# A spread of gating jobs over TensorE's order, switched off in a list schedule

## The chip, the cores and the metric

The kernel runs on one core of a Trainium2 chip. The metric is the time of one execution in microseconds; several executions are made and their median is taken. A hardware profile of one execution shows what each engine did: TensorE (PE, with its weight loads as PEld), VectorE (DVE), ScalarE (ACT), GpSimd (POOL), SyncE (SP, which here only issues transfers) and the 16 DMA engines.

## The reference

A gated linear recurrence over 4 sequences of 5,824 tokens with 256 channels, and behind it a multiplicative feed-forward network (FFN) of width 1,024 on all 23,296 tokens.

```python
log_a = c * sig_r * np.log(np.clip(a_base, 1e-06, 1.0 - 1e-06))[None, None, :]
a_t = np.exp(log_a)
norm = np.sqrt(np.maximum(1.0 - a_t * a_t, 1e-06))
x_gated = norm * sig_i * x
for t in range(S):
    h = a_t[:, t] * h + x_gated[:, t]
    y[:, t] = h
...
a = x @ w1
b = x @ w2
h = a * b @ w3
return (h @ w_out).astype(np.float32)
```

Here `sig_r` and `sig_i` are sigmoids of the two gates, and the `x` of the network is the recurrence's `y`.

## The kernel before

**Chunks.** The tokens are cut into 46 chunks: one of 256 tokens and 45 of 512 (L48). Each chunk goes through two halves.

**The gating half.** Three loads on SP's queue bring r, i and x (`load`, L106). ScalarE takes the tanh of both gates (`tanh_r`, `tanh_i`). GpSimd adds 1 and multiplies by x (`plus`, `times`). Two transposes bring channels onto partitions (`turn_r`, `turn_u`; for chunks from 7 on they are DMA transposes issued by SP, L162). ScalarE makes the decay with two exponentials (`decay`, L170), GpSimd squares it (`square`, L177), ScalarE takes the root (`root`, L182), VectorE multiplies (`gated`, L187) and runs the recurrence in two scans, one for each half of the channels (`scan`, L202). GpSimd casts the result to bf16 as `y_t` (`cast`, L210).

**The FFN half.** For each of four column blocks `mp`, TensorE makes `pa` and `pb` in PSUM (`up`, L218), ScalarE copies `pa` to `sa` (`copy`, L225), VectorE multiplies `sa` by `pb` into `g_t` (`product`, L232). Then TensorE multiplies by the folded product of w3 and w_out (`down`, L239), ScalarE copies the result out of PSUM (`evac`, L245) and SP stores it (`store`). `pa` and `pb` share three PSUM buffers (tag `pab`, L67), so TensorE can be no more than three blocks ahead of `copy` and `product`. The text calls the FFN half of chunk c "row c"; its four products are p0 to p3.

**Groups.** tanh and exponential use one ScalarE table and the root another. So the roots of a group of chunks (`group_sizes`, L53: groups of four from chunk 10 on) stand together, and each group costs two table loads. The groups from chunk 10 on begin at chunks 10, 14, 18, 22, 26, 30, 34, 38 and 42.

**The order.** A list schedule in Python (L293 to L500) decides the program order on every engine before the program is built. Each step is a job with an engine, an assumed duration and a due time; at each moment an engine takes the first job, in order of due time, that is startable: inputs done, buffer free. Engines then execute their queues strictly in this order. `EVEN = 10` (L85) adds one more condition for groups whose first chunk is at least 10: the dictionary `hold` (L326 to L348) names, for each gating job, a matmul job that must have begun first (L436). For ScalarE's gating jobs these are spread, in proportion to their durations, over the sixteen `pa` jobs of four rows; for `gated`, the two `scan`s and `cast` of chunk c they are the `pb` jobs 0 to 3 of row c − 2 (`AHEAD = 2`).

```python
        total = sum(d for d, _ in ops)
        acc = 0.0
        for d, key in ops:
            pos = first + min(npos - 1, int(npos * (acc + d / 2) / total))
            hold[key] = ("pa", pos // 4, pos % 4)
            acc += d
        for c in g:
            for mp, key in enumerate((("gated", c), ("scan", c, 0), ("scan", c, 1), ("cast", c))):
                hold[key] = ("pb", c - AHEAD, mp)
```

Of the kernel before, what the change touches and what calls it, by code (L numbers as in the profile page):

```python
# [20 lines left out]
def kernel(  # L21
# [60 lines left out]

    T = {}

    EVEN = 10  # L85
    AHEAD = 2
    NPE = 7
    NDV = 3
# [238 lines left out]
    for k, g in enumerate(groups):  # L327
        if g[0] < EVEN:
            continue
# [205 lines left out]
```

## Time and profile before

| what | us |
|---|---|
| median of 7 executions (572.45 to 574.19) | 573.51 |
| the profiled execution, whole | 573.51 |
| its span, first to last instruction | 571.7 |
| TensorE busy | 502.7 |
| ScalarE busy | 463.1 |
| VectorE busy | 456.4 |
| GpSimd busy | 322.3 |
| first `sa` copy of row 9 | 145.7 |
| first `sa` copy of row 41 | 511.8 |

The span is what the profile shows; 1.8 us of the execution's time lie around it. The last two lines mark the stretch in which the gating of the groups that begin at chunks 10 to 38 meets the FFN: the gated steps and scans of the group that begins at chunk g stand in rows g − 1 to g + 2. Row starts are found by counting `sa` copies, four to a row.

### The profile page before, as it was taken

The numbers are of one execution on the slowest core, as the hardware profiler recorded it, in microseconds if no ns is written. First come the engines' busy times: TensorE is split into PE (matmuls) and PEld (weight loads), VectorE is DVE, ScalarE is ACT, GpSimd is POOL, SyncE is SP. The second block draws the span as 40 slices with busy tenths as digits, with TensorE's granted clock in tenths as the row PEclk, the third lists the DMA queues.
The fourth block names the chain that finished last, engine by engine and source line by source line (L and its number), as shares of the span: only waits on it lengthen the run. The fifth ranks groups of instructions, "written<-read, shape, count | busy, mean of one in ns | idle before, by whom it ended". The sixth has DMA issues, their size and how long they took to land.

```text
span 571.7 us, 8497 instructions
## 1 busy us (share of the span) xinstructions
PE 502.7 (88%) x3104; PEld 304.2 (53%) x3160; DVE 456.4 (80%) x355; ACT 463.1 (81%) x539; POOL 322.3 (56%) x196
## 2 busy tenths in 40 slices
PE   1479898978987999998997997898999899789997
PEld 1346665644654655655554554564565565455565
DVE  1877468497899799799699699789879879978852
ACT  6696899997986988988987897798889799666543
POOL 6124975769197268449558649707926937821000
PEclk9989999989999999999999999999999999999999
DMA  9996799999988859949979989797995993321112
GB/s 219 253 308 179 198 332 253 289 258 246 282 234 229 231 162 277 285 135 272 238 222 250 221 250 205 224 249 184 278 275 148 239 284 106 91 56 56 37 56 92
DMA packets 183897, 120.10 MB, mean 210 GB/s; under 512 B 86576, under 2 KB 182832, under 8 KB 183856
## 3 DMA queue, kind: packets, MB, share of 16 engines
q1 hardware_dynamic: 179216, 115.89, 75.8%
q0 software_dynamic: 4368, 3.67, 3.9%
q8 instruction: 24, 0.39, 0.3%
q14 instruction: 17, 0.14, 0.1%
q10 hardware_dynamic: 272, 0.00, 0.0%
HBM read 78.91 MB, written 23.86 MB: 180 GB/s over the span
## 4 chain that ended last, share of the span: by engine, by line
PE 41%; DVE 20%; issue 14%; ACT 4%; POOL 1%; DVEq 0%; POOLq 0%; ACTq 0%
PE pa L218 15%; PE pb L218 13%; PE po L239 13%; DVE h_t L202 9%; DVE g_t L232 9%; DVE nrm L187 2%; ACT L170 1%; ACT sa L225 1%; ACT ot L245 1%; ACT a_t L170 1%; POOL y_t L210 1%; ACT nrm L182 0%; ACT L182 0%; DVEq L232 0%; POOLq L210 0%
## 5 line engine op out<-in xcount | busy, mean ns | idle before, releaser
L232 DVE TENSOR_TENSOR g_t<-sa,pb 128x1024 bf16<-128x1024 bf16 (+1 forms) x184 | 218.0, 1197 | 70.5 <-ACT sa L225 49.9
L225 ACT CAST sa<-pa 128x1024 bf16<-128x1024 f32 (+1 forms) x184 | 183.8, 1002 | 79.5 <-PE pa L218 73.0
L218 PEld LDWEIGHTS <-w_sb 128*128 128x128 bf16 x1472 | 143.7, 98 | 187.1 <-issue 33.8
L218 PE MATMUL pa<-y_t,w_sb 128*128 128x512 bf16 (+1 forms) x706 | 186.0, 379 | 37.8 <-DVE g_t L232 26.5
L218 PE MATMUL pb<-y_t,w_sb 128*128 128x512 bf16 (+1 forms) x710 | 185.3, 379 | 2.1 <-ACT sa L225 0.6
L239 PE MATMUL po<-wp_sb,g_t 128*128 128x256 bf16 x1456 | 182.8, 274 | 4.4 <-ACT ot L245 3.8
L239 PEld LDWEIGHTS <-g_t 128*128 128x128 bf16 x1456 | 143.2, 98 | 50.5 <-issue 4.9
L202 DVE TENSOR_TENSOR_SCAN h_t<-a_t,h_t,nrm 128x512 f32<-128x512 f32 (+3 forms) x90 | 156.8, 1751 | 0.7
L210 POOL CAST y_t<-h_t 128x1024 bf16<-128x1024 f32 x44 | 55.0, 1250 | 132.5 <-DVE h_t L202 132.5
L177 POOL TENSOR_TENSOR nrm<-a_t 128x1024 f32<-128x1024 f32 x43 | 90.4, 2105 | 31.7 <-ACT a_t L170 31.7
L144 POOL TENSOR_TENSOR u_t<-th_i,x_t 128x1024 bf16<-128x1024 f32 x39 | 97.5, 2500 | 2.8
L132 POOL TENSOR_SCALAR th_i<-th_i 128x1024 f32<-128x1024 f32 x43 | 61.2, 1422 | 46.6 <-ACT th_i L127 45.6
L187 DVE SCALAR_TENSOR_TENSOR nrm<-nrm,ut 128x1024 f32<-128x1024 f32 x39 | 67.7, 1737 | 12.7 <-ACT nrm L182 12.7
L245 ACT COPY ot<-po 128x512 f32<-128x512 f32 x91 | 53.0, 585 | 12.6 <-PE po L239 12.5
L170 ACT ACTIVATE a_t<-rt,la 128x512 f32<-128x512 bf16 x78 | 62.1, 816 | 0.1
L127 ACT ACTIVATE th_i<-i_t 128x1024 f32<-128x1024 f32 (+1 forms) x46 | 48.2, 1047 | 1.3 <-DMA i_t<-in_i_gate_dram 1.3
L182 ACT ACTIVATE nrm<-nrm 128x1024 f32<-128x1024 f32 (+1 forms) x46 | 47.2, 1053 | 2.4 <-DVE nrm L177 1.2
L120 ACT ACTIVATE th_r<-r_t 128x1024 bf16<-128x1024 f32 x39 | 41.4, 1064 | 0.0
L182 ACT ACT_TABLE_LOAD x15 | 19.2, 1283 | 0.3
L152 PE MATMUL ptr<-ident,th_r 128*128 128x128 bf16 x52 | 4.8, 245 | 12.8 <-DVE ident L73 8.7
L170 ACT ACT_TABLE_LOAD x12 | 15.4, 1283 | 0.8 <-DVE la L285 0.6
L187 DVE SCALAR_TENSOR_TENSOR nrm<-nrm,ptr 128x1024 f32<-128x1024 f32 (+1 forms) x7 | 8.0, 1137 | 5.9 <-ACT nrm L182 5.9
(33 smaller groups left out, 103.7 us busy)
## 6 DMA issues: line engine op xcount, KB each, us to landing
out_dram<-ot SPq DMA_DIRECT2D x91, 256.0 KB, 3.2
r_t<-in_r_gate_dram SPq DMA_DIRECT2D x45, 512.0 KB, 5.3
i_t<-in_i_gate_dram SPq DMA_DIRECT2D x45, 512.0 KB, 5.3
x_t<-in_x_dram SPq DMA_DIRECT2D x45, 512.0 KB, 5.2
w_t<-in_moe_w_dram POOLq DMA_DIRECT2D x8, 256.0 KB, 17.0
w_sb<-in_moe_w_dram POOLq DMA_DIRECT2D x8, 128.0 KB, 9.9
rt<-th_r SPq DMA_TRANSPOSE x39, 4.3
ut<-u_t SPq DMA_TRANSPOSE x39, 4.6
```

What stands on the lines that cost most here:

```text
L132: nc.gpsimd.tensor_scalar(t, t, 1.0, 1.0, op0=ALU.add, op1=ALU.mult)
L144: nc.gpsimd.tensor_mul(out=u.rearrange("p cb j q -> p j cb q"), in0=cut(t), in1=cut(T["x", c]))
L170: nc.scalar.activation(out=T["a", c][:, cb, :w], in_=T["pr", c][:, cb, :w], func=AF.Exp, scale=la4[:, cb:cb + 1], bias=la4[:, cb:cb + 1])
L177: eng.tensor_mul(out=t[:, :, :w], in0=T["a", c][:, :, :w], in1=T["a", c][:, :, :w])
L182: nc.scalar.activation(out=T["n", c][:, :, :w], in_=T["n", c][:, :, :w], func=AF.Sqrt, scale=-1.0, bias=1.0)
L187: nc.vector.scalar_tensor_tensor(out=T["n", c][:, :, :w], in0=T["n", c][:, :, :w], scalar=1e-3, in1=T["pu", c][:, :, :w], op0=ALU.max, op1 ...
L202: nc.vector.tensor_tensor_scan(T["h", c][:, cb, lo:hi], T["a", c][:, cb, lo:hi], T["n", c][:, cb, lo:hi], init, ALU.mult, ALU.add)
L210: eng.tensor_copy(out=T["y", c][:, :, :w], in_=T["h", c][:, :, :w])
L218: nc.tensor.matmul(out=pp[:, q, :w], lhsT=w_sb[:, cb, m * P:(m + 1) * P], rhs=T["y", c][:, cb, :w], start=(cb == 0), stop=(cb == NCB - 1))
L225: nc.scalar.copy(out=sa[:, :, :w], in_=T["pa", c, mp][:, :, :w])
L232: nc.vector.tensor_mul(out=T["g", c][:, 2 * mp:2 * mp + 2, :w], in0=T["sa", c, mp][:, :, :w], in1=T["pb", c, mp][:, :, :w])
L239: nc.tensor.matmul(out=T["po", c, j // 2][:, j % 2, :], lhsT=T["g", c][:, k, j * P:(j + 1) * P], rhs=wp_sb[:, k, :], start=(k == 0), stop= ...
```

## The change

The constant goes from 10 to 100. There are 46 chunks, so no group qualifies any more, `hold` stays empty, and the condition at L436 never applies. Nothing else differs: the same jobs with the same durations and due times are scheduled.

```diff
-    EVEN = 10
+    EVEN = 100
```

The same instructions come out on every engine; up to row 8 their order is the same too. Behind it, VectorE's order per group is this, from the group's first gated step to its last scan (g a gated step, s a scan, p an FFN product; the spaces are only for reading):

```
before, groups at 10, 26:  g p p g s p s p s p g p s p s p s p g p s p s
before, groups at 14, 30:  g p s p g p s p s p g p s p p s s p p g s p p s
before, groups at 18, 34:  g s p p g s p p s g p p s p s p g s p p s s
before, groups at 22, 38:  g p g p s s p p s g p p s s p p s g p s p s
after, group at 10:        g p p g s p s p g p s p s p g p s p s p s p s
after, groups at 14, 18:   g p s p g p s p g p s p s p g p s p s p s p s
after, groups at 22 to 38: g s p p g s p g p s p s p g p s p s p s p s
```

The order before repeats every 16 chunks, the order after (from chunk 22) every four. On ScalarE the changed order from chunk 22 on has, in the row of the roots, the first exponential of the next group ahead of that row's last `sa` copy; and `tanh_r` and `tanh_i` of the group's second chunk stand one row later than before in most groups. GpSimd's order changes little: in some groups `times` and `square` of neighbouring chunks swap. SP's loads, transposes and stores keep their number and move by a few places among each other.

## The prediction

> **What bounds the kernel now.** I read the page's busy shares first, then its chain of waits.
>
> ```profile
> PE 502.7 (88%) x3104; PEld 304.2 (53%) x3160; DVE 456.4 (80%) x355; ACT 463.1 (81%) x539; POOL 322.3 (56%) x196
> PE 41%; DVE 20%; issue 14%; ACT 4%; POOL 1%; DVEq 0%; POOLq 0%; ACTq 0%
> PE pa L218 15%; PE pb L218 13%; PE po L239 13%; DVE h_t L202 9%; DVE g_t L232 9%; DVE nrm L187 2%; ACT L170 1%; ACT sa L225 1%; ACT ot L245 1%; ACT a_t L170 1%; POOL y_t L210 1%; ACT nrm L182 0%; ACT L182 0%; DVEq L232 0%; POOLq L210 0%
> ```
>
> The chain runs through TensorE, and where it leaves TensorE it goes mostly to VectorE's scans and products. ScalarE is as busy as VectorE but hardly on the chain. So I cut the stretch from row 9 to row 41 into its eight groups and asked for the busy time of each engine in each; columns are window, length, then PE, PEld, DVE, ACT, POOL.
>
> ```profile
> 145.70:192.20 46.50, 41.34 (x245) 24.13 (x248) 42.42 (x32) 39.32 (x48) 29.80 (x16) 1.00 0.83 228
> 192.20:237.30 45.10, 42.82 (x257) 25.38 (x260) 39.09 (x29) 39.58 (x48) 28.41 (x16) 1.00 0.94 247
> 237.30:282.00 44.70, 42.18 (x255) 25.05 (x258) 38.24 (x28) 39.41 (x48) 29.62 (x16) 1.00 0.84 222
> 282.00:328.10 46.10, 42.27 (x257) 25.21 (x260) 39.70 (x30) 39.19 (x48) 29.45 (x16) 1.00 0.90 236
> 328.10:374.50 46.40, 41.38 (x245) 24.08 (x248) 42.32 (x30) 39.27 (x47) 29.80 (x16) 1.00 0.85 221
> 374.50:419.60 45.10, 42.82 (x257) 25.37 (x261) 39.08 (x29) 39.58 (x48) 28.41 (x16) 1.00 0.95 239
> 419.60:464.30 44.70, 42.17 (x255) 25.05 (x258) 38.27 (x30) 39.41 (x47) 29.62 (x16) 1.00 0.87 228
> 464.30:511.80 47.50, 41.41 (x249) 24.43 (x253) 42.33 (x29) 36.57 (x45) 25.96 (x14) 1.00 0.44 121
> ```
>
> These are the groups at 10, 14, ... 38; together 366.1 us. The same order takes the same time twice (46.5 and 46.4, 45.1 and 45.1, 44.7 and 44.7), so an order has a price. The length follows DVE's busy time: 42.4 goes with 46.5, 38.2 with 44.7. ScalarE's is alike in the first seven, whatever the length.
>
> Why does DVE's busy time differ, with equal work? The timeline inside the group at 26 (start, duration, engine) shows it:
>
> ```profile
> 350.66 1.19 DVE L232 TENSOR_TENSOR g_t<-sa,pb 128x1024 bf16<-128x1024 bf16 x1
> 351.67 2.35 POOL L144 TENSOR_TENSOR u_t<-th_i,x_t 128x1024 bf16<-128x1024 f32 x1
> 351.77 3.33 DVE L187 SCALAR_TENSOR_TENSOR nrm<-nrm,ut 128x1024 f32<-128x1024 f32 x1
> 355.02 1.21 DVE L232 TENSOR_TENSOR g_t<-sa,pb 128x1024 bf16<-128x1024 bf16 x1
> 355.96 1.89 POOL L177 TENSOR_TENSOR nrm<-a_t 128x1024 f32<-128x1024 f32 x1
> 356.16 2.77 DVE L202 TENSOR_TENSOR_SCAN h_t<-a_t,h_t,nrm 128x512 f32<-128x512 f32 x1
> 358.85 1.19 DVE L232 TENSOR_TENSOR g_t<-sa,pb 128x1024 bf16<-128x1024 bf16 x1
> 359.86 2.35 POOL L144 TENSOR_TENSOR u_t<-th_i,x_t 128x1024 bf16<-128x1024 f32 x1
> 359.97 3.32 DVE L202 TENSOR_TENSOR_SCAN h_t<-a_t,h_t,nrm 128x512 f32<-128x512 f32 x1
> ```
>
> A gated step takes 1.22 us and a scan 1.28 alone (their medians), a product 1.2 always. Here POOL starts a step of 1.9 to 2.35 us during each product, just before DVE starts its gated step or scan, and that one lasts until POOL's step is over and its own time has passed on top: 3.33 = 2.25 + 1.1. Undisturbed, a group's DVE work is 16 × 1.21 + 4 × 1.22 + 8 × 1.28 = 34.5 us; the table's mean is 40.2. So 5.7 us of each group are such waits, and where they are many, products and the PSUM buffers behind them come late and TensorE waits.
>
> **The change part by part.** *Instructions.* None is added or removed: the kernels hold the same jobs. All cost lies in the order, from row 9 on; what comes ahead (145.7 us) costs 0.
>
> *VectorE.* What differs among the orders listed with the change is how often a gated step or scan stands right behind a single product, the place where the timeline shows the long waits. Counted per group of 12 such steps, single-product places are 9 in the orders of 46.5 and 46.4 us, 6 at 45.1, 2 at 44.7, but 4 at 46.1 and 47.5. The changed order has 9 in the group at 10, 11 in those at 14 and 18, and 8 in those at 22 to 38, whose last eight steps alternate strictly with products, as in the group at 26. The nearest row is therefore the order with 9: (46.5 + 46.4) / 2 = 46.45 a group, and eight make 371.6. Against 366.1 that is **+5.5 us**. The bounds are the cheaper rows: 45.1 × 8 = 360.8, or −5.3; and the dearest, 47.5 × 8 = 380.0, or +13.9. I take 46.4, rounded down since 8 is a little under 9: 371.2, **+5.1**.
>
> *ScalarE.* A group's work is 8 tanh at 1.06, 8 exponentials at 0.816, 4 roots at 1.05, 16 copies at 1.0, 8 evacuations at 0.585 and 2 table loads at 1.283: 8.5 + 6.5 + 4.2 + 16.0 + 4.7 + 2.6 = 42.5, in either kernel. Moved ahead of the last `sa` copy in the roots' row are a table load and an exponential, 1.28 + 0.82 = 2.1 us. The product behind that copy comes 2.1 us later, but in VectorE's changed order a gated step (1.22) stands ahead of it, and by the next row's first copy both orders have done the same set. So I take 0; uncovered, it is 2.1 − 1.22 = 0.9 a group, +7 over eight. One new wait: `tanh_r` of the group's second chunk now stands a copy (1.0), a tanh (1.07), an evacuation (0.6) and a copy (1.0) ahead of its exponential, 3.7 us, and the DMA transpose between them lands 4.3 us after its issue. The exponential can wait 0.6 us, and behind it in ScalarE's queue the other exponential and the row's last copy. VectorE, late by its waits there, covers it; I take 0, at most 0.6 × 6 = +3.6.
>
> *SP, DMA, POOL.* Loads land in a median of 5.3 us, and ScalarE waited 1.3 us in all for loads of i; with the same buffers and moves of a few places I take 0, up to 5.3 once if a load becomes late. POOL's swaps of a 2.35 and a 1.89 us step are in the group's price. *The last group.* From row 41 to the end takes 571.7 − 511.8 = 59.9 us, TensorE busy nearly throughout. The group at 42 alternates once in the changed order, and POOL's products and squares are over by then, so its scans run at 1.28 us: 0, within 1.5 either way.
>
> *Sum.* 573.5 + 5.1 = **578.6 us** for an execution of which the profiled one, 573.51, is the median of the seven.
>
> **The rivals.** *The alternation does no harm (faster).* At the start of each row the changed order has finished the same VectorE steps as the orders at 18 and 34, the cheapest; only the places inside a row differ, and a product after each step frees PSUM buffers sooner. Then groups cost 45.1 (the order with 6 single places) or less: 360.8 in all, 573.5 − 5.3 = 568.2 us; at 44.7 it is 565.0. For it: single places alone don't order the rows (6 is cheaper than 4). Against: both orders that alternate over long runs are among the dear ones. It decides if POOL has no step ready when the lone product ends.
>
> The Trainium skill bears on this rival: its page "SBUF — State Buffer", section "Who interferes with whom", has VectorE steps with two SBUF inputs and GpSimd steps exclude each other, whichever began first for the whole instruction. With POOL's phase taken as even, a wait behind a product is half a POOL step (an estimate: 0.8 us, from 1.04, 2.35, 1.89 and 1.04) and behind another such VectorE step a whole one, 1.6. Counting places, the changed order from 22 on would then wait 2 × 1.6 + 10 × 0.8 = 11.2 us a group and the old ones on average 3 × 1.6 + 9 × 0.8 = 12.0; by 1.75 us of length for 4.1 of DVE time (first and third row above) that is −0.3 a group, 571 us. The trace agrees with the exclusion (3.33 us) but not with the even phase: POOL began 0.10 to 0.20 us ahead of the waiting step three times in a row. I go by the row.
>
> *Nothing measurable.* A reshuffle without a better or worse order on average: eight groups at the mean of 45.8, 573.5 us. For it: the four old orders are themselves a mixture, and the work is the same. Against: the new order is one order repeated, and single orders differ by 2.8 us.
>
> *ScalarE too.* The 2.1 us ahead of the last copy and the late exponential are not covered, and come on top of VectorE's waits: 47.5 a group, 587.4 us. Against: the old profile shows VectorE waiting for `sa` 49.9 us in all, mostly in rows without gating.
>
> **How the numbers follow.** Within 0.2%, 1.1 us either way, I call it the same, about what measurements of this kernel can tell. The forecast with its neighbours above 574.7 has 0.52, ScalarE too 0.10, nothing measurable 0.13, the faster rival (with the even phase) 0.25. So slower 0.62, same 0.13, faster 0.25. Since cases of both signs hold most of the chance: the forecast's own range is 575 to 583 (46.0 to 46.9 a group). For 8 in 10 the range reaches down to 569.0, which cuts off the cheaper half of the faster rival, and up to 585.5, which cuts off the dearer half of ScalarE too.
>
> **What would show it.** Right: scans and gated steps from row 9 to 41 busier than before (the page's means are 1.75 and 1.74 us), DVE busy above 41 us in each group window, the groups alike and near 46.4, and TensorE's idle time ahead of `pa` released by `g_t` above 26.5 us. Wrong: scans nearer 1.5 us and groups under 45.1; or groups long with DVE at 39 to 40 us, which would put it on ScalarE, with `sa` waits and idle time ahead of L170 released by the transposes. If the time before row 9 or after row 41 moves by more than 2 us, the division itself is wrong.

## The result, and the profile after

The changed kernel takes 575.05 us in the median of 17 executions (574.28 to 579.27), the kernel before 573.13 us (44 executions, 571.53 to 575.0). The ratio is 1.0042, 95% interval 1.0032 to 1.0053: the change makes the kernel 0.4% slower. The direction is the one forecast; the size is less than half of it.

The page of the changed kernel: busy times, the chain of waits by engine, the lines of scans and gated steps (lines left out are marked).

```profile
PE 502.5 (88%) x3104; PEld 304.9 (53%) x3160; DVE 461.2 (81%) x355; ACT 462.8 (81%) x539; POOL 323.1 (56%) x196
PE 51%; DVE 18%; issue 6%; ACT 3%; POOL 1%; DVEq 0%; POOLq 0%; ACTq 0%
...
L202 DVE TENSOR_TENSOR_SCAN h_t<-a_t,h_t,nrm 128x512 f32<-128x512 f32 (+3 forms) x90 | 170.5, 1899 | 0.8
...
L187 DVE SCALAR_TENSOR_TENSOR nrm<-nrm,ut 128x1024 f32<-128x1024 f32 x39 | 58.7, 1508 | 12.0 <-ACT nrm L182 12.0
```

The same two lines in the kernel before:

```profile
L202 DVE TENSOR_TENSOR_SCAN h_t<-a_t,h_t,nrm 128x512 f32<-128x512 f32 (+3 forms) x90 | 156.8, 1751 | 0.7
L187 DVE SCALAR_TENSOR_TENSOR nrm<-nrm,ut 128x1024 f32<-128x1024 f32 x39 | 67.7, 1737 | 12.7 <-ACT nrm L182 12.7
```

Three engines are as busy as before within 0.3 us (PE, ACT) and 0.8 us (POOL); VectorE has 4.8 us more. It is not spread evenly: a scan now takes 1.90 us on average (1.75 before), a gated step 1.51 (1.74 before).

The busy time of each engine in the eight groups from row 9 to row 41 (window, length, then PE, PEld, DVE, ACT, POOL), cut at the changed kernel's own row starts:

```profile
144.30:189.60 45.30, 41.72 (x251) 24.69 (x254) 40.66 (x32) 39.41 (x47) 29.65 (x16) 1.00 0.89 244
189.60:234.00 44.40, 41.64 (x253) 24.83 (x255) 38.98 (x29) 38.41 (x47) 28.65 (x16) 1.00 0.88 247
234.00:278.60 44.60, 42.74 (x258) 25.36 (x261) 39.22 (x29) 39.45 (x47) 29.66 (x16) 1.00 0.89 224
278.60:325.50 46.90, 42.15 (x254) 24.86 (x257) 41.57 (x31) 39.24 (x47) 29.40 (x16) 1.00 0.85 227
325.50:372.70 47.20, 41.87 (x254) 24.92 (x257) 41.88 (x29) 39.40 (x47) 29.65 (x16) 1.00 0.87 222
372.70:419.90 47.20, 42.02 (x253) 24.87 (x257) 41.87 (x29) 39.38 (x47) 29.65 (x16) 1.00 0.86 220
419.90:467.10 47.20, 42.03 (x253) 24.91 (x257) 41.97 (x31) 39.40 (x48) 29.65 (x16) 1.00 0.86 224
467.10:513.50 46.40, 41.67 (x252) 24.82 (x255) 39.85 (x29) 37.81 (x46) 24.74 (x14) 1.00 0.50 126
```

The sum is 369.2 us against 366.1. The groups at 10 and 14 became cheaper (46.5 to 45.3, 45.1 to 44.4), the one at 18 stayed, those at 22 to 34 cost up to 2.5 us more, the last 1.1 less. From row 41 to the end the changed kernel takes 59.1 us, 0.8 less than before. The stretch ahead of row 9 is 1.4 us shorter in this one execution. Up to row 7 its order is the same in both kernels (in row 8 TensorE's and ScalarE's already differ), and already row 1 starts 0.9 us earlier (32.4 against 33.3 us). Four kernels of the experiments below with the changed order up to there (`late`, `skip_first`, `early`, `skip_second`) reach row 9 at 144.8 to 145.8 us, against 145.7 before and 144.3 here. So most of the 1.4 us belongs to the executions, not to the change.

VectorE's waits can be read off as busy time, since a waiting step is recorded as a longer one. In these windows stand 32 gated steps and 64 scans' worth of work, which alone take 32 × 1.22 + 64 × 1.28 = 121.0 us. They took 121.6 + 58.4 = 180.0 us before and 135.8 + 48.5 = 184.3 us after: waits of **59 us before and 63 us after**. The text below calls this number "the waits".

Groups 18 and 26 show what decides. From the group's third gated step on, their VectorE order is the same, one after the other. First the group at 18 (start, duration, engine; lines of other engines are left out here and in the timelines below):

```profile
249.71 1.05 POOL L132 TENSOR_SCALAR th_i<-th_i 128x1024 f32<-128x1024 f32 x1 [3.26 <-ACT th_i L127]
249.75 1.19 DVE L232 TENSOR_TENSOR g_t<-sa,pb 128x1024 bf16<-128x1024 bf16 x1
250.84 3.47 POOL L144 TENSOR_TENSOR u_t<-th_i,x_t 128x1024 bf16<-128x1024 f32 x1
250.86 1.21 DVE L187 SCALAR_TENSOR_TENSOR nrm<-nrm,ut 128x1024 f32<-128x1024 f32 x1
```

Then the same place in the group at 26:

```profile
340.32 1.84 POOL L132 TENSOR_SCALAR th_i<-th_i 128x1024 f32<-128x1024 f32 x1 [2.39 <-ACT th_i L127]
341.24 1.19 DVE L232 TENSOR_TENSOR g_t<-sa,pb 128x1024 bf16<-128x1024 bf16 x1
342.24 2.36 POOL L144 TENSOR_TENSOR u_t<-th_i,x_t 128x1024 bf16<-128x1024 f32 x1
342.35 3.33 DVE L187 SCALAR_TENSOR_TENSOR nrm<-nrm,ut 128x1024 f32<-128x1024 f32 x1
```

In the first the two long steps come up 0.02 us apart; VectorE's takes 1.21 us and GpSimd's `times` waits (3.47 = 1.12 + 2.35), although its record starts first: a lead this small in the records doesn't say who wins. In the second `times` comes 0.11 us first and VectorE waits 2.1 us. Why so close a race, again and again? GpSimd's `plus` takes about 1.0 us once it can run, VectorE's product 1.2. Both begin when a scan ends. So GpSimd's next step comes up just before VectorE's. In the group at 18 `plus` began only when its tanh was done; it ends 0.18 us ahead of the product's end there, 0.27 us in the group at 26, and this 0.09 us decides. Places where VectorE waited over 0.3 us for a `times` that had begun less than 0.3 us earlier, with a product as VectorE's step before and `plus` as GpSimd's, number 11 before and 18 after. They hold 22 us of the waits before and 37 us after. The sum rises by 4 us only, for the other waits fall: all waits for `times` go from 29 to 40 us, those for `square` from 23 to 21, for `plus` from 4 to 2 and for `cast` from 3 to 0.

### The profile page after: what moved, and what is told of

Its sections match the earlier page's. It is cut to its first block, busy times and chain, and to the rows that moved or that the text cites. A ratio compares the mean times of both kernels' runs of the same rounds, so it can differ in the third digit from the quotient of the medians.

```text
span 572.6 us, 8493 instructions
## 1 busy us (share of the span) xinstructions
PE 502.5 (88%) x3104; PEld 304.9 (53%) x3160; DVE 461.2 (81%) x355; ACT 462.8 (81%) x539; POOL 323.1 (56%) x196
## 4 chain that ended last, share of the span: by engine, by line
PE 51%; DVE 18%; issue 6%; ACT 3%; POOL 1%; DVEq 0%; POOLq 0%; ACTq 0%
PE pa L218 18%; PE po L239 16%; PE pb L218 16%; DVE h_t L202 11%; DVE g_t L232 7%; DVE nrm L187 1%; ACT sa L225 1%; ACT ot L245 1%; ACT a_t L170 1%; POOL u_t L144 1%; ACT L170 0%; ACT nrm L182 0%; POOL y_t L210 0%; POOL nrm L177 0%; POOL th_i L132 0%
## 5 line engine op out<-in xcount | busy, mean ns | idle before, releaser
L218 PE MATMUL pa<-y_t,w_sb 128*128 128x512 bf16 (+1 forms) x703 | 185.5, 380 | 39.9 <-DVE g_t L232 33.4
L202 DVE TENSOR_TENSOR_SCAN h_t<-a_t,h_t,nrm 128x512 f32<-128x512 f32 (+3 forms) x90 | 170.5, 1899 | 0.8
L132 POOL TENSOR_SCALAR th_i<-th_i 128x1024 f32<-128x1024 f32 x43 | 64.0, 1489 | 62.8 <-ACT th_i L127 61.9
L144 POOL TENSOR_TENSOR u_t<-th_i,x_t 128x1024 bf16<-128x1024 f32 x39 | 95.9, 2460 | 3.1
L187 DVE SCALAR_TENSOR_TENSOR nrm<-nrm,ut 128x1024 f32<-128x1024 f32 x39 | 58.7, 1508 | 12.0 <-ACT nrm L182 12.0
L170 ACT ACTIVATE a_t<-rt,la 128x512 f32<-128x512 bf16 x78 | 61.8, 814 | 0.1
L182 ACT ACTIVATE nrm<-nrm 128x1024 f32<-128x1024 f32 (+1 forms) x46 | 47.2, 1054 | 2.3 <-DVE nrm L177 1.1
```

Of the source, the lines that this page charges most:

```text
L132: nc.gpsimd.tensor_scalar(t, t, 1.0, 1.0, op0=ALU.add, op1=ALU.mult)
L144: nc.gpsimd.tensor_mul(out=u.rearrange("p cb j q -> p j cb q"), in0=cut(t), in1=cut(T["x", c]))
L170: nc.scalar.activation(out=T["a", c][:, cb, :w], in_=T["pr", c][:, cb, :w], func=AF.Exp, scale=la4[:, cb:cb + 1], bias=la4[:, cb:cb + 1])
L182: nc.scalar.activation(out=T["n", c][:, :, :w], in_=T["n", c][:, :, :w], func=AF.Sqrt, scale=-1.0, bias=1.0)
L187: nc.vector.scalar_tensor_tensor(out=T["n", c][:, :, :w], in0=T["n", c][:, :, :w], scalar=1e-3, in1=T["pu", c][:, :, :w], op0=ALU.max, op1 ...
L202: nc.vector.tensor_tensor_scan(T["h", c][:, cb, lo:hi], T["a", c][:, cb, lo:hi], T["n", c][:, cb, lo:hi], init, ALU.mult, ALU.add)
```

## The experiments

The theory after the result is the **race theory**: VectorE's gated steps and scans and GpSimd's steps that read SBUF exclude each other, an order's price is set mainly by how many of these races VectorE loses, and tenths of a microsecond decide that. Rivals: the **counting theory** of the prediction (the number of steps behind single products sets the price) and the **ScalarE theory** (moved exponentials and tanh).

### Without three of GpSimd's reading steps: `nl_before`, `nl_after`

These kernels leave out GpSimd's `plus`, `times` and `square`. GpSimd's `cast`, which reads too, stays, and so does the square of the first three chunks, which VectorE makes. The code is shortened.

```diff
 def plus(c):
-    nc.gpsimd.tensor_scalar(t, t, 1.0, 1.0, op0=ALU.add, op1=ALU.mult)
+    pass
 def times(c):
-    nc.gpsimd.tensor_mul(out=u.rearrange("p cb j q -> p j cb q"), in0=cut(t), in1=cut(T["x", c]))
+    nc.gpsimd.memset(u, 0.5)
 def square(c):
-    eng.tensor_mul(out=t[:, :, :w], in0=T["a", c][:, :, :w], in1=T["a", c][:, :, :w])
+    if c < NDV:
+        nc.vector.tensor_mul(out=t[:, :, :w], in0=T["a", c][:, :, :w], in1=T["a", c][:, :, :w])
 def root(c):
-    nc.scalar.activation(out=T["n", c][:, :, :w], in_=T["n", c][:, :, :w], func=AF.Sqrt,
+    nc.scalar.activation(out=T["n", c][:, :, :w], in_=T["n" if c < NDV else "a", c][:, :, :w], func=AF.Sqrt,
```

> The kernel before with GpSimd's steps that read SBUF taken out except the cast: plus is left out, times is a fill of u with a constant, square is left out (the root reads the decay itself). The order of all that stays is the same. Exclusion theory: scans fall to about 1.3 to 1.5 us on average, the eight groups from row 9 to 41 differ by less than 0.7 us in place of 2.8, and the total falls to about 555 to 562 us. If TensorE's or ScalarE's order made the groups differ, they still differ by 2 us or more.

> The changed kernel with the same three GpSimd steps taken out. Exclusion theory: within 1.5 us of the kernel before without them, the difference of 1.9 us between the two orders gone or turned, and all groups alike. If ScalarE's moves (the exponential ahead of the last copy, the later tanh) cost time, the changed order stays at least 2 us slower.

Measured: 535.07 us with the order before (ratio to the kernel before 0.9342, 0.9318 to 0.9366) and 535.94 with the changed one (0.9350, 0.9327 to 0.9373): no difference between the orders that these runs can tell. Both fell further than expected. The costliest gated and scan groups of `nl_after`, then one of its windows (the group at 26; the one at 30 takes 41.6 us too):

```profile
L199 DVE TENSOR_TENSOR_SCAN h_t<-a_t,h_t,nrm 128x512 f32<-128x512 f32 (+3 forms) x90 | 112.8, 1258 | 0.8
L184 DVE SCALAR_TENSOR_TENSOR nrm<-nrm,ut 128x1024 f32<-128x1024 f32 x39 | 47.5, 1220 | 12.0 <-ACT nrm L179 12.0
```

```profile
307.60:349.20 41.60, 41.60 (x259) 25.03 (x257) 33.13 (x29) 38.95 (x47) 7.83 (x8) 1.00 1.01 256
```

The waits are gone (scans 1.26 us, gated steps 1.22), and TensorE is busy for the whole window: the groups are TensorE's own 41.6 us. In `nl_before` the eight add up to 332.6 us, here to 333.1. They still differ by 1.6 us in `nl_before` (40.8 to 42.4, TensorE busy throughout), against the 0.7 expected, since the cuts at row starts hold more or fewer matmuls; the group at 26, dear before at 46.4, is among the cheapest there. ScalarE's moved exponential and tanh, which stay in this pair, cost no more than about 0.5 us over the eight groups here. Since TensorE was busy throughout, a small delay of ScalarE could hide behind it, so this pair alone bounds their price only for a kernel without the waits.

### One step of one chunk: `skip_second`, `skip_first`

```diff
+    SKIP = (27, 31, 35, 39, 43)      # skip_first: (26, 30, 34, 38, 42)
 def plus(c):
+    if c in SKIP:
+        return
 def times(c):
+    if c in SKIP:
+        T["u", c] = gates.tile([P, NCB, 4, P], BF16, name="u_t", tag="u")
+        nc.gpsimd.memset(T["u", c], 0.5)
+        return
```

> The changed kernel; for chunks 27, 31, 35, 39 and 43 (the second chunk of the next group) GpSimd's plus is left out and times is a fill with a constant, which reads nothing. Everything else in the same order. Race theory: these are the steps that begin 0.1 us ahead of the gated step of the group's fourth chunk; without them it takes 1.22 us in place of 3.33, and groups 22 to 34 fall from 47.2 to 44.7 us or less: total 562 to 566 us (changed kernel 575). If one lost race is made up elsewhere, 573 to 575 us.

> The changed kernel with the same two GpSimd steps left out for chunks 26, 30, 34, 38 and 42 (the first chunk of the next group) in place of the second. As much GpSimd work is gone. Race theory: in the changed kernel these steps run while VectorE has only products or waits for the root, and no gated step or scan waits for them: 574 to 575.5 us, groups 22 to 34 still at 47 us. If it is the amount of GpSimd work that sets the time, as much is gained as with the second chunk: 562 to 566 us.

Measured: 554.24 us without the second chunk's steps (ratio to the kernel before 0.9661, 0.9640 to 0.9683), 575.52 without the first chunk's (1.0037, 1.0024 to 1.0050). The same amount of GpSimd work is taken out; in one place it is worth 21 us against the changed kernel, in the other nothing. In `skip_first` the groups at 26 to 34 stay at 47.2 us. In `skip_second` the group at 26 is:

```profile
322.70:365.30 42.60, 41.98 (x259) 24.96 (x257) 37.27 (x29) 39.15 (x47) 25.08 (x15) 1.00 0.95 240
```

42.6 us in place of 47.2, more than the one wait of 2.1 us, and the total falls below the 562 to 566 us expected: VectorE is 4.6 us less busy, so the later races of the group turn with the first one (18 in all become 5).

### The same steps moved: `late`, `early`

`put(key, behind)` takes a step out of the program order and puts it right behind another one; each run has one of the two lines.

```diff
+    for c in (27, 31, 35, 39, 43):
+        put(("tanh_i", c), ("evac", c - 7, 1))     # late: one evacuation later
+        put(("tanh_i", c), ("tanh_r", c))          # early: one copy earlier
```

> The changed order, with one edit: tanh_i of chunks 27, 31, 35, 39 and 43 (the second chunk of the next group) stands one evacuation (0.59 us) later in ScalarE's order. Nothing else moves. Race theory: in the changed kernel GpSimd's times step of that chunk begins 0.1 us ahead of VectorE's gated step of the group's fourth chunk, which then waits 2.1 us, and later waits follow from it; with times 0.6 us later the gated step begins first, and groups 22 to 34 fall from 47 us to the 44.6 us of group 18, which has the same order: total about 575 - 11 = 564 us. Counting theory (the prediction's): the VectorE order, and so the number of steps behind single products, is the same, so the time stays at 575 us within 1. ScalarE theory: a copy or an exponential moves by half a microsecond, within 1 us of 575.

> The changed order, with the same five tanh_i one copy (1.0 us) earlier in ScalarE's order. Race theory: times begins 1.0 us earlier, so the gated step still loses but waits only about 1.3 us of the 2.35 us step in place of 2.1; groups 22 to 34 at 46 to 47 us, total 571 to 575 us. Counting theory: 575 us within 1.

`late` missed: 575.95 us (ratio 1.0051, 1.0032 to 1.0070), the changed kernel's time, which both rivals had expected. Its timeline in the group at 26 says why:

```profile
340.86 1.27 DVE L202 TENSOR_TENSOR_SCAN h_t<-a_t,h_t,nrm 128x512 f32<-128x512 f32 x1
341.62 1.34 POOL L132 TENSOR_SCALAR th_i<-th_i 128x1024 f32<-128x1024 f32 x1 [2.88 <-ACT th_i L127]
342.05 1.19 DVE L232 TENSOR_TENSOR g_t<-sa,pb 128x1024 bf16<-128x1024 bf16 x1
343.05 2.35 POOL L144 TENSOR_TENSOR u_t<-th_i,x_t 128x1024 bf16<-128x1024 f32 x1
343.16 3.33 DVE L187 SCALAR_TENSOR_TENSOR nrm<-nrm,ut 128x1024 f32<-128x1024 f32 x1
```

`plus` did come half a microsecond later, but it had been waiting for the scan anyway (1.84 us in the changed kernel, 1.34 here). It ends at the same point of the group, and `times` still leads by 0.11 us. The shift was within the slack. `early` gave 569.02 us (0.9927, 0.9898 to 0.9956), 0.7% faster than the kernel before. It moved the way that the race theory said, but further than the 571 to 575 us expected:

```profile
338.15 1.04 POOL L132 TENSOR_SCALAR th_i<-th_i 128x1024 f32<-128x1024 f32 x1 [1.48 <-ACT th_i L127]
338.78 1.48 DVE L202 TENSOR_TENSOR_SCAN h_t<-a_t,h_t,nrm 128x512 f32<-128x512 f32 x1
339.27 3.13 POOL L144 TENSOR_TENSOR u_t<-th_i,x_t 128x1024 bf16<-128x1024 f32 x1
340.18 1.19 DVE L232 TENSOR_TENSOR g_t<-sa,pb 128x1024 bf16<-128x1024 bf16 x1
341.29 2.20 DVE L187 SCALAR_TENSOR_TENSOR nrm<-nrm,ut 128x1024 f32<-128x1024 f32 x1
```

`times` is under way earlier, and the gated step waits 1.0 us in place of 2.1. The races go from 18 to 12 and the waits from 63 to 57 us. VectorE's order is unchanged, so the counting theory, which expected 575 us within 1, falls here.

### More work for GpSimd: the fills

```diff
 def plus(c):
     nc.gpsimd.tensor_scalar(t, t, 1.0, 1.0, op0=ALU.add, op1=ALU.mult)
+    if c >= 10:
+        nc.gpsimd.memset(gap, 0.0)     # gap: a tile of its own, 128x128 or 128x512
```

The narrow fill stands behind `cast` too, and so does the wide one in `pad_wide2`.

> The changed kernel with work added: behind each plus and each cast of chunks from 10 on GpSimd fills a 128x128 tile with zeros (0.2 us), which nobody reads. Race theory: plus or cast (1.04 us) fits into one product (1.19 us), so GpSimd's next, long step begins about 0.1 us before VectorE's next one and makes it wait some 2 us, 18 times behind plus; with 0.2 us more, VectorE comes first. Waits from row 9 to 41 fall from 63 us to 35 to 45, total 560 to 568 us: more work, less time. Counting theory and ScalarE theory: 575 us or more (up to 7 us more, 72 fills of 0.2 us, where GpSimd is on the path).

> The kernel before with the same added fills. Race theory: 11 such races behind plus and 3 behind cast in place of 18 and 6, so the gain is smaller: 564 to 570 us, and within 3 us of the changed kernel with the fills. Otherwise 573 us or more.

Both missed: 577.50 us (1.0073, 1.0055 to 1.0092) and 575.64 (1.0032, 1.0020 to 1.0044), which the rivals allow. The waits did not fall (65 and 61 us). The fill of 0.20 us moved `times` by only 0.03 us: it begins 0.11 us behind the end of `plus` in place of 0.08, and still 0.08 us ahead of the gated step. So the dose was raised:

> The changed kernel with a wider fill behind each plus of chunks from 10 on (128x512, about 0.5 us, none behind cast). The narrow fill lay in the gap between GpSimd's steps: times still began 0.08 us ahead of the gated step or scan. Race theory: now VectorE begins 0.2 to 0.3 us ahead of times, the races behind plus turn, waits from row 9 to 41 fall from 63 us to 30 to 45, and the total to 558 to 570 us although GpSimd has 18 us more work. If VectorE's gain is given back because GpSimd then waits and casts come late: 573 to 580 us, with fewer waits of VectorE but TensorE waiting for y_t. If the races are not what the order costs: waits and time stay at 63 and 575 or more.

> The kernel before with the same wide fill behind plus. Race theory: 12 waits of over 1.9 us turn in place of 19, so less is gained than in the changed kernel: waits from 59 to 35 to 45 us, total 560 to 570 us; the two orders then within 3 us of each other. If GpSimd becomes late: 573 to 580 us.

Measured: **555.43 us** with the changed order (0.9689, 0.9672 to 0.9706) and 566.85 us with the order before (0.9884, 0.9854 to 0.9913). The page's line of the fills in `pad_wide`, and the known place in its group at 26:

```profile
L135 POOL MEMSET gap<- 128x512 f32 x36 | 18.9, 524 | 0.0
```

```profile
337.57 0.52 POOL L135 MEMSET gap<- 128x512 f32 x1
337.82 1.21 DVE L190 SCALAR_TENSOR_TENSOR nrm<-nrm,ut 128x1024 f32<-128x1024 f32 x1
338.06 3.19 POOL L147 TENSOR_TENSOR u_t<-th_i,x_t 128x1024 bf16<-128x1024 f32 x1
```

Now VectorE leads by 0.24 us, and `times` waits. 18.9 us of useless fills make the changed kernel 20 us faster. The waits fall from 63 to 43 us with the changed order, and from 59 to 52 with the old one. None of the races described above is left in either (18 and 11 before). The old order has fewer of them to turn; it stays 11 us behind, which is more than the 3 us expected, and its waits stay above the expected 35 to 45 us.

> The changed kernel with the wide fill behind each plus and also behind each cast of chunks from 10 on. Behind cast the long step is square; 17 waits of 1.3 us on average, 21.7 us in all, were for it. Race theory: many of them turn too, waits from row 9 to 41 fall from 43 us (fill behind plus alone) to 25 to 35, total 548 to 554 us against 555.4. If square, now later, makes the roots late, or GpSimd's 19 us more work put it on the path: 556 to 562 us.

553.85 us (0.9656, 0.9620 to 0.9693), the fastest of the kernels that leave nothing out, but not told apart from `pad_wide`, whose interval overlaps. The waits are 40 us, not the 25 to 35 expected. The fill behind `cast` does turn what it was meant for: against `pad_wide`, the waits for `square` fall from 22 to 11 us. But those for `times` rise from 18 to 25 us and those for `plus` from 3 to 5, so little is left in the sum.

### A planner that knows of the exclusion: `lock_free`

```diff
+        if key[0] in LOCKED and locked[0] > t:
+            return False
...
+            if key[0] in LOCKED:
+                locked[0] = start + dur
```

Here `LOCKED` names `gated`, `scan`, `plus`, `times`, `square` and `cast`, and their durations were set to those alone.

> The changed kernel's list schedule with the exclusion modelled: gated, scan, plus, times, square and cast share one resource, with the durations that the trace shows alone (plus 1.05, times 2.35, square 1.9, cast 1.05, scan 1.28), so the planner puts a product where VectorE would wait. The order changes everywhere. Race theory: waits of gated steps and scans below 45 us, total 555 to 570 us, if ScalarE and TensorE follow; the planned order is irregular, so 575 to 580 us is possible, then with few VectorE waits and more waits of TensorE for y_t.

566.19 us (0.9876, 0.9847 to 0.9904). The waits from row 9 to 41, summed step by step over those above 0.3 us, fall to 45 us, but the order is irregular: the groups take 41.6 to 47.2 us, and row 9 starts at 151.3 us, some 6 us later than in the others (the new rule acts on the first chunks too). It is faster than the kernel before and the changed one. The run sets two things at once, the exclusion and the durations, so which of them helped is not shown.

## Why the prediction was right or wrong

**What bounds the kernel** held. The length of a group goes with VectorE's waits for GpSimd, and without the three reading steps TensorE runs without a gap and the two orders can't be told apart. The waits are larger than the prediction's 5.7 us a group: step by step they are 59 / 8 = 7.4 us, since the records of neighbouring VectorE steps overlap a little and the busy time counts the overlap once. And each column block takes two of the three `pab` buffers, so TensorE can be only one and a half blocks ahead, not three; a late product reaches it soon.

**VectorE's term** is the step that failed, in size and in its reason. The prediction had read the long waits rightly and even saw that GpSimd began 0.10 to 0.20 us ahead, three times in a row, but it priced each group by "how often a gated step or scan stands right behind a single product", took the row with 9 such places, 46.4 us, for all eight, and came to +5.1 us. The eight took 45.3, 44.4, 44.6, 46.9, 47.2, 47.2, 47.2 and 46.4 us, +3.1. The groups with the most single places, 11 at 14 and 18, are the cheapest, those with 8 the dearest. What the runs showed in its place: a single product behind a scan is only the occasion. The long wait for `times` comes if GpSimd has a short step and then that long one pending there, since 1.0 us is over before 1.2 is; `early` changed the price of an order of VectorE without touching that order, and `pad_wide` turned the dearest groups (47.2) into 43.6 us ones. Such races rose from 11 to 18, about 15 us more, but other waits shrank by some 10 us, which the prediction had no term for. That the rows with 6 and 4 places were out of line had been in the prediction's own count.

**The direction** was right partly by luck. The alternating stretch in the groups from 22 on did lose races as the timeline of the prediction shows it, and these groups carry the loss. But by the count the groups at 14 and 18 would have been dearer still, and they turned out cheapest. Of the signs named for being right, scans got busier (1.75 to 1.90 us) and TensorE's idle time for `g_t` ahead of `pa` rose (26.5 to 33.4 us). Gated steps got shorter (1.74 to 1.51 us), VectorE is above 41 us in only four of the eight windows, and the groups are not alike.

**ScalarE at 0** is borne out: 0.5 us between the two orders in the `nl` pair, with the reserve said there, and `pad_wide`, which keeps ScalarE's changed order, is 11 us ahead of the old order with the same fill. The feared late exponential didn't show either; the page after has 0.1 us of idle time ahead of the exponentials (L170), as before. One reason given against the rival with ScalarE was too strong: of VectorE's 49.9 us of waits for `sa`, 22.8 lie in rows 9 to 41, where there is gating.

**SP, DMA, POOL at 0**: nothing in the runs speaks against it, but no run tried it by itself. GpSimd's own waits for `th_i` rose from 45.6 to 61.9 us in the waits of the whole execution, off the path.

**The last group at 0, within 1.5**: −0.8 us. Together: +3.1 − 0.8 = +2.3 us in the profiled executions apart from the stretch ahead of row 9, beside +1.9 between the medians.

**The faster rival** was lost for this change but for its condition. It was to decide "if POOL has no step ready when the lone product ends". With the wide fill GpSimd's long step is not ready then, and the alternating order is 11 us better than the old one. Its second estimate took the phase as even and gave −2.7 us over the eight groups. The phase is not even: 18 of the 21 waits for `times` began within 0.3 us of it. The exclusion itself, which that estimate took from the Trainium skill ("SBUF — State Buffer", "Who interferes with whom"), is what `nl_after` shows: the waits are gone, and 23 gated steps and scans that ran beside a fill, which reads nothing, took their 1.22 and 1.28 us.

**Nothing measurable** was close in size. The intervals tell 0.42% from it.

## What to carry to other kernels

Where VectorE and GpSimd steps exclude each other, look at who comes first at each meeting, not at how much work there is: compare the start times in the timeline to a tenth of a microsecond. Where GpSimd wins again and again by 0.1 us with a step twice as long, delaying it by more than that margin, or taking its reading out there, can be worth more than a new plan: here the wide fill gave 20 us, and the one plan tried that knows of the exclusion 9 us (575.05 to 566.19). A list schedule that doesn't know of the exclusion leaves such margins to chance, and moving a constant of it then picks one order among many. That is my reading; only two values of this constant were run.

## What the runs showed that was not expected

- A fill of 0.20 us behind `plus` delayed `times` by 0.03 us: its record overlaps the end of `plus` and the start of `times`. One of 0.52 us delayed it by 0.35 us and turned the race.
- Adding 18.9 us of work to GpSimd took 20 us off the time (575.05 to 555.43).
- The product of `sa` and `pb`, one input of which is in PSUM, took 1.18 to 1.22 us in chunks of 512 tokens in every run here, whatever GpSimd did beside it.
